# Two zero products for TensorE, K and R scaled by one instruction, and a new order behind the start

## The chip, the cores and the metric

The kernel runs on one core of one Trainium2 chip. The metric is the device time of one execution in microseconds; the kernel before was executed three times and the median counts. Traces come from one more execution under the profiler; its span runs from the first to the last instruction of the program.

## The reference: what is computed

Two layers follow one another.

The first is a linear attention with decay: batch 4, 8 heads, 768 steps, head width 48. For each head a 48 x 48 state is carried along the steps:

```python
cur   = einsum('bhd,bhe->bhde', u * k[t], v[t])
y[t]  = einsum('bhd,bhde->bhe', r[t], state + cur)
state = w * state + einsum('bhd,bhe->bhde', k[t], v[t])
```

The second takes y as x, 3072 rows of 384: `h = relu(x @ w_in)` (384 to 1024 columns), a convolution over three neighbouring steps per column, `gate = sigmoid(conv)`, and `(h * gate) @ w_out` (1024 to 384). The inputs come as 64-bit numbers for the two weight matrices and the convolution, as float32 otherwise.

## The kernel before, in words

**The attention part** works on 24 groups (6 for each batch) of 128 steps, each group two chunks of 64 steps. For each group g `load` issues the transfers of K and R with the head width on the partitions (one tile `KR`, K in its half 0, R in its half 1), of K and R with time on the partitions (`KV`), and of V. `prep` (line 379) scales K and R by powers of the decay: two VectorE products (lines 384 to 386, recorded under the helper's line 208), each of 112 x 512 elements, one for K by `TK`, one for R by `TR`. `TK` and `TR` are the halves of one tile, `TKR`, which ScalarE and VectorE fill at the start (lines 320 to 323). For g below 4 `prep` also transposes K with small TensorE products ("kt", line 394) and sums u*k*r with others ("q", line 407); later groups do this on VectorE and GpSimd. Then come three families of small TensorE products, all recorded under line 495: scores (K by R, into `psA` or a bank lent by the other layer), additions to the state (K by V), and outputs (`psY`, scores by V and R by state). For g below 4 they are the separate operations VA, VU and VY, later one operation V of 64 or so interleaved products. `chain` masks the scores into `RS` (line 512) and carries the state (`SS`, `SD`); `split` cuts y into a high and a low part for the second layer (`XT`, lines 549 and 550).

**The second layer** runs in 7 units of up to 510 steps, 8 blocks of 128 columns each, so 56 blocks. `first(i)` makes 9 TensorE products (line 581) of up to 512 columns into one of two banks `HP`. ScalarE takes the relu and the middle tap (lines 585, 586), VectorE the two outer taps (line 589), ScalarE the sigmoid (592), VectorE the product with h (593), ScalarE the high part `GH` (595) and VectorE or GpSimd the low part `GL`. The bank is free for block i + 2 when line 593 has read it. `second(i)` makes three times 3 products (line 610) into the three banks `PO`, which are copied out and stored after the eighth block. The 16 weight pieces are converted from 64-bit numbers along the way (lines 349 to 365).

**The start** is a list of its own: `warm` (line 274) makes 40 products of a zero tile `wz` into banks that nobody uses yet, 5 with 512 columns and 35 with 104.

**What sets the order.** Each call of `op` records an operation with its engines, an assumed duration and what it reads and writes. Nothing is scheduled in the kernel: `Plan.order` reads the list `ORDER`, one number for each operation, with a letter where an operation that may run on several engines gets one (a: ScalarE, d: VectorE, p: GpSimd). The operations are then issued in that order, and each engine works through its own share of it, first in, first out. All transfers are issued by SyncE, in the order of the list too.

Of the kernel before, what the change touches and what calls it, by code (L numbers as in the profile page):

```python
# [11 lines left out]
ALU = mybir.AluOpType  # L12
# [4 lines left out]
C = 64  # L17
NP = H // 2
# [34 lines left out]
FN = 256  # L53
# [3 lines left out]
26 17 0 8 12 15 10 1 16 4 21 14 9 5 27 11 20 2 23 18 22 43 13 33 35 19 3 31 44 37 32 50 34 55 82 38 56 81 28 39 64 29  # L57
59d 40 41 36 72 57 6 30 73 60 76d 45 77 46a 52d 58a 47 208 74 207 48 61 7 49d 84a 65 51 63d 83 78 62a 85 230 80p 214
88 66 67 229 68a 53 42 75d 54 69p 103 90 210a 70 104 86 209 92d 107d 236 89 211 100 91 212 108 71a 87d 215 213d 105 93
109 79a 216d 110p 232a 95d 276 112 217 106a 277 111d 231 113 98 126 96 233 94a 97p 218 127 115 237 219p 283 114 116a  # L60
238d 124 99 299 24 234 25 117 239 298 278 279d 125 131 118a 240 280 119a 241d 235d 140 155d 121 123 281 158d 101 130
149 120 150 134p 122 102 132 146 148 285a 147 284 156d 198 301a 343 286 300 282d 305 133a 302 287 344 220 153 199 129
154 200 128 303 201 350 135 304p 221 202 152 222 138 157 142p 136 203 223 288p 137a 139 204 224 175p 267 143 170 173
151 225 144a 176p 226 141 268 289 159p 269 145 177 307a 270 227 160 162p 306 271 346a 369 308 272 174 169 290 273 345
205 228d 375 334 291 347 171 352a 206d 368 166 163 292 351 164p 168 313 167 274 178p 413 312 335 165 172 309 161 311
182p 336 357 293 275p 348 180 337 294 179a 349p 338 295 353 356 189 310d 339 359 193d 256 370 340 196p 187 184 181 188
371a 358 183 194p 377a 431 185 404 296 186 191 376 360 192 414 361 297d 242 405 378 354 372 406 362 355p 373 407 382
381 379 247 383 258 259 363 248 195 251 253 249 252 364 341 365 262p 374p 419 420 422 254 250 190 257 197p 408 342d
437 438 421 439 415a 380d 416 244 245a 409 366 433a 432 423 367p 470 471 469 410 411 424 243 263d 425 426 427 264 246
266a 324 323 255 428 434 260 329d 261 332d 460 461 417 462 463 464 472 435 473 474 475 476 465 466 412p 265p 314 322  # L70
393 325 326 418p 483 316p 330p 331 429 320 321 315 317 327 328 318d 319 430p 436p 482 481 513 525 522 528 399d 400p
333a 477 514 515 516 517 478 384 396 392 450 449 394 401 531 386p 526 523 518 467 390 387 388a 519 520 391 385 532 533
398 389 397 534 535 468p 541 561 402p 440 503 451 452 395 502 448 479 562 563 564 536 529 537 565 480p 538 566 442p
453 454 443 446 403a 540 542 573 572 521p 584 574 575 508d 567 604 605 606 444p 445 447 441 682 455p 494 576 458p 484
492 504 530 501 490 456p 457 607 608 577 491 578 579 568 569d 486a 487 509p 511p 539p 570 571 583 582 615 616 617 618
459p 493 506 507 488p 489 614 626 613 625 627 485 543 609 619 610 545d 556p 580 581d 658 510 620 621 497 505 496 495
499 524 500 498 648 551 550 599p 659 557d 555 554 622 512a 547 611 612p 649 650 546 544 548 623 651 652 558 653 549
593 594 654 598 660 661 662 663 664 559p 670 585 592 552 597 600p 624p 665 587 590 666 701 702 703 655 671 713 719 657
669 588p 560p 589 591 601 603a 586 602p 553 527 595 628 636 704 705 720 706 641 656d 721 707 722 723 637 691 596 638
690 714 630p 631 632d 716 729 710 717 724 634 667 711 751 752 753 725 763 668d 643d 629 635 761 694 708 764 765 754  # L80
755 642 728 730 762 633 646d 672 689 692 726 756 757 758 795 644p 709p 674p 766 767 768 746p 696p 678 679 645 683 688
685 640 741 686 693 639 687 675 684 740 759d 647a 796 797 769 770 773 774 760 772 807 808 809 727p 805 673 676d 798
744 799 800 680 677 697d 698 695 681 817 806 804 747p 749p 699p 733p 810 801 811 812 731 737 784 739 745 813 748 734
735a 771d 837 838 839 814 849 700p 738 736 732 777d 840 790d 793p 791p 850 841 851 842 852 843 802 803d 775 789 778
816 818 888 848 847 846 779p 815p 788 853 792 844 750a 854 855 889 890 781 776 794d 780 782 845d 906 907 908 856 909
742 712 715 827 821p 743 819 859 858 860 903 900 910 820 911 912 891 823 913 892 783 785 830 893 822 894 950 897 938
951 952 895 832p 833d 834 835d 826 883p 886p 857p 831 824 896p 953 954 955 787 786 861 901 939 868 866 877 828 825 878
718 956 836p 862 940 881 941 942 867 873 871 876 872 870 928 829 927 898 863 904 994 995 915 947 917 916 943 944 945
884d 946d 885 864d 882 865 982 1176 957 958p 914p 996 983 984 985 986 932 997 933d 987 988 869 887a 948 960 959 949
961 991 993 1003 918 924 934p 920p 998 936d 935 977d 980p 999 1000 1001 879 992 1004 880 899 874 875 1026 1038 921  # L90
922p 931 919 923 1027 1028 937p 964d 925 962 1036 926 930 971 972 902 929 1029 1030 1039 1031 989 990p 978p 1002d 1032
1040 1041 1042 965 976 966d 1043 979 1074 1035 1005 1037 1049 1044 1095 1091 1047 1033 1075 1076 968 1077 975 1078 969
1079 967 963 1096 1097 1080 1098 1034p 1021p 1016 905 1015 973 974 970 1006 1012 1008p 981p 1014 1007 1009 1010d 1099
1100 1081 1045 1020 1011 1019 1101 1046d 1024p 1069d 1070p 1060 1048 1087 1083 1088 1017 1092 1093 1084 1107 1108 1102
1109 1125 1110 1013 1071 1111 1126 1127 1112 1082d 1113 1128 1129 1106 1105 1117 1104 1114 1050 1073p 1056 1086 1089
1137 1116 1130 1057 1131 1103p 1149 1134 1146 1138 1139 1072d 1022d 1140 1141 1094 1064 1090 1085 1061 1132 1150 1058
1151 1142 1143 1052p 1068 1133d 1152 1053 1153 1115p 1154 1155 1158 1135 1147 1062 1063 1065 1066 1118 1144 1145p 1159
1171 1161 1162 1163 1023 1025d 1164 1165 1059 1067 1136 1148 1160 1183 1166 1193 1167 1184 1195 1054p 1055 1018 1051
1119 1185 1156 1121d 1186 1157p 1172 1170 1207 1192 1204 1187 1188 1189 1213 1196 1168 1197 1198 1199 1200 1122 1123
1190 1208 1214 1169p 1120 1124 1173 1215 1205 1174 1201 1225 1194 1210 1223 1175 1179 1206 1216 1217 1218 1222 1219  # L100
1237 1191p 1234 1235 1226 1227 1211 1220 1202 1228 1229 1221p 1230 1231 1238 1239 1240 1241 1203d 1249 1250 1251 1252
1242 1243 1253 1224 1244 1232 1254 1247 1246 1236 1248 1233d 1255 1245d 1256 1261 1259 1262 1263 1264 1265 1266 1267
# [56 lines left out]
def rwkv_ffn_kernel(tc, krd, krt, vt, wd, ut, w_in, conv_w, w_out, out):  # L159
# [3 lines left out]
    op = plan.op  # L163
    with ExitStack() as ctx:
# [496 lines left out]
        for i in range(NU * NF + LAG):  # L661
            x = (i + LEAD) / NF
# [80 lines left out]
```

## Time and profile before

| what | value |
|---|---|
| runs shown, us | 294.24, 296.36, 297.02 (median 296.36) |
| profiled execution, its own time | 296.27 us |
| its span, first to last instruction | 294.5 us |
| TensorE (PE) busy | 280.2 us, 95% |
| VectorE (DVE) busy | 242.0 us, 82% |
| ScalarE (ACT) busy | 191.5 us, 65% |
| GpSimd (POOL) busy | 114.8 us, 39% |
| moved by DMA | 37.47 MB, mean 127 GB/s |
| mean granted clock of TensorE | 0.994 |

Busy time is the time in which an instruction of the engine runs; TensorE's is of matrix products alone, its weight loads (PEld) overlap with them. The ends of products are modelled, so a short wait between two can hide in a busy stretch. "Issue" is a wait for which the profile shows no cause. A granted clock of 1.00 is 2.4 GHz, 0.50 is 1.2 GHz.

### The profile page before, as it was taken

Reading aid. Unit: us, or ns where it says so; the run is one execution under the profiler, and the core shown is the slowest. Engines: PE = TensorE matmul, PEld = TensorE weight load, DVE = VectorE, ACT = ScalarE, POOL = GpSimd, SP = SyncE. Lnnn points to the kernel's source line nnn. Section 1 sums busy time; section 2 is a strip of 40 time slices with the busy share of each in tenths; the row PEclk is TensorE's granted clock in tenths of the full one; section 3 lists DMA queues with packets and bytes.
Section 4 is the critical chain, followed back from the end, with each engine's and each line's share of the span. In section 5 each row is a group of like instructions: output and inputs, shape, how many; then the busy total and the mean of one; then the engine's idle time right before and its main releaser. Section 6 shows DMA issues by size and latency. Waiting matters only on the chain.

```text
span 294.5 us, 10385 instructions
## 1 busy us (share of the span) xinstructions
PE 280.2 (95%) x4368; PEld 242.6 (82%) x4368; DVE 242.0 (82%) x439; ACT 191.5 (65%) x452; POOL 114.8 (39%) x143
## 2 busy tenths in 40 slices
PE   8769799999999999998999999999999999999995
PEld 6669788889989988886888878888888888889895
DVE  5867999999998989998997987888798973565561
ACT  3446699997887566866496566464853555656662
POOL 4112164565577635166337333645150340112100
PEclk9979999999999999999999999999999999999999
DMA  7987998977455673435364508643413001200121
GB/s 174 225 193 198 234 227 227 241 167 176 120 159 161 168 199 118 118 82 154 90 202 129 157 2 186 191 147 87 146 44 61 2 4 45 92 0 0 38 71 56
DMA packets 18642, 37.47 MB, mean 127 GB/s; under 512 B 3874, under 2 KB 10532, under 8 KB 18596
## 3 DMA queue, kind: packets, MB, share of 16 engines
q1 hardware_dynamic: 18596, 36.82, 48.0%
q8 instruction: 34, 0.56, 0.8%
q14 instruction: 12, 0.10, 0.1%
HBM read 30.01 MB, written 4.72 MB: 118 GB/s over the span
## 4 chain that ended last, share of the span: by engine, by line
PE 46%; DVE 18%; issue 9%; ACT 9%; POOL 7%; DMA 7%; SPq 4%; POOLq 0%; ACTq 0%
PE PO L610 17%; PE HP L581 16%; DVE CV L589 6%; PE psY L495 5%; SPq L212 4%; DMA KV<-in_krt_dram 4%; POOL KV L208 4%; DMA ST<-in_w_in_dram 3%; DVE SG L593 2%; POOL GL L208 2%; DVE KR L208 2%; ACT CV L586 2%; DVE XT L550 2%; ACT HP L585 1%; ACT SG L592 1%
## 5 line engine op out<-in xcount | busy, mean ns | idle before, releaser
L581 PE MATMUL HP<-XT,wi 128*128 128x512 f32 (+3 forms) x504 | 111.5, 367 | 2.9 <-DVE SG L593 1.4
L581 PEld LDWEIGHTS HP<-XT,wi 128*128 128x128 f32 x504 | 88.0, 188 | 18.6 <-DVE SG L593 3.7
L610 PE MATMUL PO<-GH,wo 128*128 128x510 f32 (+3 forms) x336 | 101.9, 363 | 0.0
L589 DVE SCALAR_TENSOR_TENSOR CV<-HP,cw,CV 128x510 f32<-128x510 f32 (+3 forms) x112 | 74.9, 672 | 17.6 <-ACT CV L586 15.8
L610 PEld LDWEIGHTS PO<-GH,wo 128*128 128x128 f32 x336 | 61.4, 188 | 8.6
L208 POOL TENSOR_TENSOR GL<-SG,GH 128x510 fp32r<-128x510 f32 (+3 forms) x31 | 36.4, 1175 | 66.1 <-ACT GH L595 64.2
L610 PE MATMUL PO<-GL,wo 128*128 128x510 f32 (+3 forms) x168 | 60.6, 361 | 0.0
L592 ACT ACTIVATE SG<-CV 128x510 f32<-128x510 f32 (+3 forms) x56 | 32.0, 571 | 43.0 <-DVE CV L589 42.7
L495 PE MATMUL psY<-RS,KV 64*48 64x64 f32 x720 | 42.9, 220 | 0.4 <-issue 0.4
L593 DVE TENSOR_TENSOR SG<-HP,SG 128x510 f32<-128x510 f32 (+3 forms) x56 | 34.2, 611 | 11.0 <-ACT SG L592 10.3
L585 ACT ACTIVATE HP<-HP 128x512 f32<-128x512 f32 (+3 forms) x56 | 29.4, 525 | 19.3 <-PE HP L581 16.8
L495 PE MATMUL psY<-KR,SS 48*48 48x64 f32 x660 | 39.8, 215 | 1.1 <-issue 1.1
L595 ACT CAST GH<-SG 128x510 fp32r<-128x510 f32 (+3 forms) x56 | 30.7, 554 | 8.5 <-DVE SG L593 7.3
L586 ACT ACTIVATE CV<-HP,cw 128x510 f32<-128x510 f32 (+3 forms) x56 | 35.1, 628 | 1.3
L610 PEld LDWEIGHTS PO<-GL,wo 128*128 128x128 f32 x168 | 31.6, 188 | 3.7
L208 DVE TENSOR_TENSOR KR<-KR,TKR 112x512 f32<-112x512 f32 x48 | 34.2, 724 | 0.1
L495 PEld LDWEIGHTS psY<-RS,KV 64*48 64x48 f32 x720 | 31.9, 120 | 0.9 <-issue 0.9
L495 PEld LDWEIGHTS psY<-KR,SS 48*48 48x48 f32 x660 | 30.2, 119 | 1.2 <-issue 1.2
L495 PEld LDWEIGHTS psA<-KR 48*64 48x64 f32 x704 | 22.3, 135 | 6.5 <-issue 2.6
L495 PE MATMUL psA<-KR 48*64 48x64 f32 x704 | 25.2, 221 | 0.2
L505 POOL TENSOR_TENSOR SD<-SS,PW 112x192 f32<-112x192 f32 x21 | 14.3, 681 | 24.5 <-DVE SS L526 8.5
L431 ACT ACTIVATE RS<-eye,QQ 128x64 f32<-128x64 f32 x80 | 20.2, 336 | 2.0 <-DVE QQ L415 2.0
(113 smaller groups left out, 351.9 us busy)
## 6 DMA issues: line engine op xcount, KB each, us to landing
KR<-in_krd_dram SPq DMA_DIRECT2D x24, 448.0 KB, 4.9
KV<-in_krt_dram SPq DMA_DIRECT2D x40, 192.0 KB, 4.2
KV<-in_vt_dram SPq DMA_DIRECT2D x48, 96.0 KB, 4.3
ST<-in_w_in_dram SPq DMA_DIRECT2D x16, 192.0 KB, 5.3
ST<-in_w_out_dram SPq DMA_DIRECT2D x8, 384.0 KB, 6.9
XT<-XT SPq DMA_DIRECT2D x24, 64.0 KB, 2.7
out_dram<-OS SPq DMA_DIRECT2D x6, 255.0 KB, 3.3
out_dram<-OS SPq DMA_DIRECT2D x3, 251.0 KB, 2.1
```

Source lines behind the costliest of these rows:

```text
L208: op(eng, d, rd, wr, lambda e: e.tensor_tensor(**kw), cls, port=True)
L431: A.activation(RS[j][:, n], eye, AF.Copy, scale=QQ[j][:, n:n + 1])
L495: PE.matmul(y, a, b_, start=s0, stop=s1)
L505: e.tensor_tensor(out=dst, in0=src, in1=PW[:, :, 64:65].broadcast_to([112, NP, D]), op=ALU.mult)
L581: PE.matmul(hp, wi[a][:, j, fs], XT[:, x, j, t], start=(j == 0 and k == 0), stop=(j == 2 and k == 2))
L585: op("act", 0.093 + n / 1200.0, [], [H_], lambda e: A.activation(hp, hp, AF.Relu, scale=1.0 / WS))
L586: op("act", 0.158 + n / 1200.0, [H_, "cw"], [("T", ti)], lambda e: A.activation(t1, hp[:, 1:n + 1], AF.Copy, scale=cw[:, 3 * f + 1:3 * f + ...
L589: op("dve", 0.117 + n * 1.085e-3, [H_, "cw"], [("T", ti)], lambda e, k=k: V.scalar_tensor_tensor(out=t1, in0=hp[:, k:n + k], scalar=cw[:, ...
L592: op("act", 0.11 + n / 1200.0, [("T", ti), "sgt"], [("SG", ti)], lambda e: A.activation(sg, t1, AF.Sigmoid))
L593: op("dve", dps(n), [H_], [("SG", ti)], lambda e: V.tensor_tensor(out=sg, in0=hp[:, 1:n + 1], in1=sg, op=ALU.mult), "GG")
L595: op("act", act(n), [("SG", ti)], [("GH", gi)], lambda e: A.copy(gh, sg))
L610: PE.matmul(PO[m][:, :n], wo[a][:, f, ms], g2[x], start=(f == 0 and k == 0), stop=(f == NF - 1 and k == 2))
```

## The change

Three edits, in one step.

1. `FILL = 2` operations are recorded right behind `warm`: each is one product of the zero tile, 128 x 128 by 128 x 512, into the bank `PO[2]`. In the new list the first stands between the second "q" and the second "kt" product group, the second between VA and VU of group 2.
2. In `prep` the two products for K and R become one product of 112 x 1024 elements, which reads all of `TKR` and so waits for all four parts of it. There are 24 such operations in place of 48.
3. The list `ORDER` is another one. With the numbers resolved to operations, the lists of the engines agree at the beginning: SyncE's first 53 transfers are the same in the same order; TensorE's first 29 operations are the same but for the two inserted ones; VectorE's first 80 or so are the same, where the merged product mostly stands at the place of the first of the two. Behind that, from about 47 us on, blocks, visits and transfers stand in another order, and some operations change their engine: in the whole list VectorE has 396 operations (433 before), ScalarE 369 (360), GpSimd 133 (129), TensorE 269 (267), SyncE 204 (204).

```diff
-FN = 256
+FN, FILL = 256, 2
 ...
 ORDER = """
-26 17 0 8 12 15 10 1 16 4 21 14 9 5 27 11 20 2 23 18 22 43 13 33 35 19 3 31 44 37 32 50 34 55 82 38 56 81 28 39 64 29
 ...
+19 0 28 14 8 17 10 9 1 18 23 4 16 5 13 29 22 25 20 2 24 15 45 21 37 3 35 33 46 39 34 52 36 82 57 81 40 30 42 41 65 31
 ...
 """
 ...
         op("pe", 2.6, ["wz"], ["o2", "o0", "psY", "psU", ("HP", 1)], warm, "warm", 6144)
 
+        for k in range(FILL):
+            op("pe", 0.2133, ["wz"], ["o2"], lambda e: PE.matmul(PO[2][:, :512], wz[:, :128], wz, start=True, stop=True), "fill", 512)
+
 ...
             kt, rt = ([(n_, i, o) for o in (0, 64)] for n_ in ("Kt", "Rt"))
-            for x, W, key, ks in ((0, TK, "K", ["TK1", "TK2"]), (1, TR, "R", ["TR1", "TR2"])):
-                v = KR[i][:, x].rearrange("q p (c t) -> q p c t", c=2)
-                tt("dve", 512, ks, [(key, i)], "KR", out=v, in0=v, in1=W.unsqueeze(2).broadcast_to([112, NP, 2, C]), op=ALU.mult)
+            v = KR[i].rearrange("q x p (c t) -> q (x p) c t", c=2)
+            tt("dve", 1024, ["TK1", "TK2", "TR1", "TR2"], [("K", i), ("R", i)], "KR", out=v, in0=v,
+               in1=TKR.rearrange("q x p t -> q (x p) t").unsqueeze(2).broadcast_to([112, 2 * NP, 2, C]), op=ALU.mult)
```

## Rows read from the trace of the kernel before

**Rows 1.** Stretches: PE, PEld, DVE, ACT, POOL busy (count), clock, DMA share, GB/s.
```profile
0.00:47.00 47.00, 39.24 (x984) 35.92 (x984) 38.20 (x82) 29.02 (x83) 14.93 (x34) 0.96 0.89 209
47.00:100.00 53.00, 51.67 (x985) 48.36 (x976) 51.14 (x99) 44.99 (x122) 33.94 (x39) 1.00 0.68 174
100.00:200.00 100.00, 98.47 (x1560) 81.51 (x1559) 90.00 (x156) 65.12 (x144) 44.95 (x49) 1.00 0.52 139
200.00:291.30 91.30, 90.81 (x854) 76.83 (x852) 62.69 (x105) 51.98 (x103) 21.01 (x23) 1.00 0.15 45
291.27:294.50 3.23, 0.00 (x0) 0.00 (x0) 0.00 (x0) 0.39 (x1) 0.00 (x0) 1.00 0.32 110
```

**Rows 2.** Timeline of PE: start, us, instructions, [idle before <- releaser].
```profile
15.94 0.49 PE L394 MATMUL HP<-DW,KR 48*64 48x48 f32 x9 [3.15 <-issue]
22.14 0.26 PE L495 MATMUL psY<-KR,SS 48*48 48x64 f32 x2 [1.09 <-issue]
30.83 0.21 PE L495 MATMUL PO<-RS,KV 64*48 64x64 f32 x1 [1.28 <-issue]
```

**Rows 3.** Stretches between and in PE's gaps of the start, columns as in rows 1.
```profile
12.80:15.94 3.14, 0.00 (x0) 0.00 (x0) 2.32 (x4) 0.73 (x4) 1.64 (x2) 1.00 1.07 231
15.94:21.06 5.12, 5.11 (x127) 4.96 (x127) 3.57 (x8) 2.06 (x7) 0.52 (x1) 0.67 0.76 165
16.60:20.00 3.40, 3.40 (x82) 3.40 (x78) 2.44 (x6) 1.97 (x6) 0.52 (x1) 0.50 0.84 183
22.14:25.69 3.55, 3.54 (x127) 3.46 (x128) 2.50 (x7) 1.12 (x4) 0.26 (x1) 1.00 0.43 135
30.83:34.59 3.76, 3.76 (x127) 3.63 (x127) 3.59 (x8) 1.47 (x5) 0.79 (x1) 1.00 0.89 223
```

**Rows 4.** The page: PE's busy us and instructions; the queue's packets, MB, share.
```profile
PE 280.2 (95%) x4368; PEld 242.6 (82%) x4368; DVE 242.0 (82%) x439; ACT 191.5 (65%) x452; POOL 114.8 (39%) x143
q8 instruction: 34, 0.56, 0.8%
```

**Rows 5.** The same queue from 12.8 to 15.94 us.
```profile
q8 instruction: 1, 0.02, 2.8%
```

**Rows 6.** Timeline of the warm-up's products; then the 512-column products of line 581.
```profile
1.69 0.63 PE L274 MATMUL psU<-wz 128*128 128x512 bf16 x1
2.12 0.63 PE L274 MATMUL HP<-wz 128*128 128x512 bf16 x1
...
L581 PE MATMUL HP<-XT,wi 128*128 128x512 f32 x288 | 72.4, 397 | 1.5 <-ACT CV L586 0.9 <-DVE SG L593 0.4 <-DMA XT<-XT 0.2
```

**Rows 7.** VectorE's products under line 208: ns min/median/max, first and last start.
```profile
L208 DVE TENSOR_TENSOR KR<-KR,TKR x48: 674/682/1980, 5.6 to 232.3; 112x512 f32<-112x512 f32 x48
L208 DVE TENSOR_TENSOR wi<-TT,wi x5: 544/550/559, 12.2 to 36.3; 128x384 fp32r<-128x384 f32 x5
```

**Rows 8.** Timeline around the first scalings of K and R.
```profile
5.49 0.30 ACT L323 COPY TKR<-TKR 112x128 f32<-112x128 f32 x1 [0.26 <-DVE TKR L320]
5.56 1.29 DVE L208 TENSOR_TENSOR KR<-KR,TKR 112x512 f32<-112x512 f32 x2
7.54 1.15 PE L495 MATMUL psA<-KR 48*64 48x64 f32 x32
8.61 0.68 DVE L208 TENSOR_TENSOR KR<-KR,TKR 112x512 f32<-112x512 f32 x1
9.30 0.17 DVE L318 TENSOR_TENSOR uw<-HP,wc 48x4 f32<-48x4 f32 x1
9.77 1.14 PE L407 MATMUL psY<-uw,KP 48*64 48x64 f32 x32
```

**Rows 9.** Waits from 47 us on: us in total, times, longest.
```profile
PE HP L581 <- DVE SG L593: 1.2, 3, 0.5
PE HP L581 <- ACT CV L586: 0.9, 1, 0.9
PEld psA L495 <- DVE KR L208: 1.2, 3, 0.5
```

More of the change, by code (lines that the diff above doesn't have):

```diff
@@ L61 @@
[L61 to L65, printed above, removed]
@@ new lines @@
+462 460 310p 259p 415 416 417 418 255 425a 407a 406 408 403 419 424 426 409 410p 247 244 246 248 245 451 308 254 252
+250 317 404p 258 387 316 420 463 474 461 472 473 452 453 427 311 454 455 322d 421 422d 456 312a 457 260p 464 465 466
+313 467 468 309 469 503 504 505 470 321 314 315 428p 515 516 518 512 458 513 519 521 522 506 507 508 323p 325p 324
+326a 523 253 319 386 318 320 377 459d 530 509 390 550 383 551 552 379p 471p 391p 380 381p 394p 392p 446p 449p 378 382
+434a 384 524 559 532 525 526 553 393 554 527 510 432 531 435 438 555 439 395p 556 511p 560 562 592 571 436a 437 385
@@ new lines @@
+760 770 725 772 701 729 704 771 768 769 811 833 834 823 824 825 826 798 835 776 836 735d 766 787p 837 761 763 838 773
+827 828p 764p 765 802 801 830 870 839 871 872 805a 873 874 767 831 842 888 829 799p 882 843 889 890 891 777p 803 809
+813 860 810 875 876 815p 816p 892 807 806 808 877 893 894 778d 818d 698 919 841 879 920 921 922 923 931 883 898 885
+932 814 804 844 861 863 812 840p 878p 933 924 865p 866p 868p 925 962 886 880 926 927p 846 847a 849 934 864 817 935 850
+853 859 857 856 910 854 855 858 909 914d 899 895 963 964 936 965 929 897 930 928 937 974 851 819a 917p 896p 867 852
@@ new lines @@
+1182 1183 1180 1181p 1172 1188 1203 1189 1204 1205 994 1046 1194 1038 1195 1202 1097 1200 1196 1206 1197 1215 1207
+1169p 1186 1101 1208 1100 1102 1098 1151 1212 1216 1217 1152 1198 1209 1227 1218 1219 1153 1201 1220 1221 1228 1210
+1229 1222 1230 1211d 1231 1199p 1232 1239 1214 1226 1213 1224 1240 1241 1233 1234 1225 1237 1236 1248 1238 1190 1155
+1160 1158 1184 1157 1159 1187 1156 1242 1243 1251 1244 1235p 1245 1263 1223p 1260 1250 1252 1253 1264 1254 1255 1265
+1256 1257 1258 1266 1267 1268 1269 1249 1262 1246 1275 1276 1277 1259d 1247d 1278 1279 1270 1271p 1280 1281 1272 1296
@@ L109 @@
+1297 1298 1299 1274 1261 1308 1284 1300 1301 1302 1309 1310 1282 1311 1312 1285 1292 1293 1313 1273 1288 1289 1290
+1303 1305 1320 1314 1321 1322 1323 1324 1306 1332 1283p 1304d 1325 1326 1317 1307 1318 1330 1333 1315 1334 1335 1336
+1327 1337 1344 1329 1319 1341 1331 1342 1345 1346 1338 1339 1328p 1316p 1353 1343 1354 1357 1355 1347 1348 1349 1350
+1340p 1360 1351 1352d 1365 1295 1286 1294 1287 1291 1366 1367 1356 1359 1362 1358 1363 1361 1364 1368 1369 1370
 """
```

77 lines of the change are left out of this document (31 added, 46 removed).

## The prediction, made before the result was known

> **What bounds the kernel now.** I read the table of stretches first, then the waits and the timeline of TensorE, then the queues. The stretches [rows 1] show two regimes. Before 47 us TensorE's products are busy 39.24 us of 47.00; from there to its last product at 291.3 us they are busy in all but 1.33 + 1.53 + 0.49 = 3.35 us, and the last 3.23 us are copying and storing out. So behind 47 us the products themselves are the bound, no order can win more than these 3.35 us and what little hides between products, and VectorE stands close behind (51.14 of 53.00 us between 47 and 100). What is large is idle in the start.
>
> The timeline shows what that idle is: TensorE stops in the middle of groups of small products for 3.15, 1.09 and 1.28 us, each time with "issue" as releaser [rows 2], so no other engine is waited for. The stretches between the gaps tell the cause [rows 3]: 127 products and 127 or 128 loads, then a stop, three times over. The page has 4368 products and 4368 loads, and 34 packets with 0.56 MB on the queue named instruction [rows 4]: 8736 / 34 = 257 instructions and 16.5 KB for each packet. One such packet falls in the gap from 12.80 to 15.94 us [rows 5]. I read these gaps as TensorE waiting for its next block of instructions. Where the DMA engines are at a share of 1.07 the gap is 3.15 us; where they are at 0.43, from 22.14 to 25.69, the stop behind is too short to stand among the three [rows 3].
>
> Now the clock. It stands at 0.50 (1.2 GHz) from 16.60 to 20.00 us and at 1.00 elsewhere in the rows [rows 3]; before it fell TensorE had been idle from 12.80 to 15.94. In these 3.40 us it was busy throughout and did the work of 1.70 us at 2.4 GHz. But the work ends at 21.06, in front of the next gap, which lasts until 22.14. If that gap ends when the block lands, a faster clock only makes it longer.
>
> Here a rule of the Trainium skill speaks otherwise. "Runtime: NRT & Kernel Launch", section Instruction fetch mechanics, says that the sequencer refills in 16 KiB blocks of 256 instructions while it executes, and that crossing a block border is mostly hidden. The trace agrees with the block's size and differs on the hiding: 3.15 us. By the rule the gaps would have another cause, nothing would fix their ends, and the sum below would hold -1.70 us for the clock in place of 0; that result is the first rival.
>
> **The change part by part.** The sum is made against the profiled execution, 296.27 us for a span of 294.5; the median of the runs shown, 296.36, is 0.09 above it.
>
> *The two zero products.* One costs between 0.25 us (72.4 us / 288 products of 512 columns) and 0.43 us (from 1.69 to 2.12 in the warm-up, at half the clock) [rows 6]; two cost 0.50 to 0.86. The first stands just ahead of the 3.15 us gap, the second, between VA and VU of group 2, ahead of the one that ends at 30.83; both only use up gap [rows 2], and they wait for nothing. I take 0; without that cover 0.86. Their four instructions move the block borders by two and four instructions, nothing at some 28 ns a product (3.55 us / 127) [rows 3].
>
> *What they give back in the clock.* Nearest row: 3.40 us at half clock [rows 3], worth up to -1.70. The first fill runs ahead of the gap and does not shorten the idle time of 12.80 to 15.94 by more than itself, so I expect the clock to fall as before in most executions. And if it does not, TensorE comes to the next border at 21.06 - 1.70 = 19.4 and waits there. I take 0, between -1.70 and +1.70: the upper end is a second fall of the same size, since 22.14 - 19.4 = 2.7 us of idle would then stand where 1.09 is now.
>
> *K and R by one instruction.* The medians of 682 ns for 512 elements and 549 for 384 [rows 7] give 1.04 ns an element and about 150 ns that do not depend on the size. One product of 1024 elements is then 150 + 1065 = 1.21 us, against 1.36 for two; the bounds are 1.18 (from the shortest, 674 and 544: 1.02 ns an element) and 1.36 (nothing saved). VectorE is relieved by some 0.15 us for each of 24 groups, 3.6 in all. At the start the product must wait for all of TKR, whose last part ends at 5.79; it then ends at about 7.0 to 7.2, still ahead of the scores at 7.54 [rows 8]: 0. The second group's product runs from 8.61 to 9.82, so uw, at 9.30 now, comes at about 9.85 and "q", at 9.77 now, a quarter of a microsecond late [rows 8]; the 3.15 us gap behind it takes that up: 0.
>
> *The order behind 47 us, and the relief of VectorE.* VectorE gets 433 - 396 = 37 operations less, 24 of them from the merging, ScalarE and GpSimd 13 more between them; TensorE's own work stays. The bounds are the idle time there: -3.35 if all of it goes, +3.35 if it doubles. Of TensorE's waits there 1.2 us end with line 593 on VectorE and 0.9 with line 586 on ScalarE [rows 9]. The relief acts on the first kind alone: I take -1.2. ScalarE, which gets nine operations more, is late next.
>
> *The moved transfers.* SyncE's first 53 are the same; behind them the order differs, where the DMA share is 0.68 and lower [rows 1]. No row shows TensorE waiting there long for a transfer: 0, within the bounds above.
>
> Sum: 0 + 0 + 0 - 1.2 = -1.2, so 296.27 - 1.2 = **295.1 us**.
>
> **The rivals.**
>
> *The clock counts (faster).* The gaps are not fixed in time, or the fills hold the clock, and the 1.70 us of the slow stretch come off in full; with 1.2 to 2.3 from the order this is 293.4 to 292.3. For it: the fall is the only one in the trace, in a stretch without any idle. Against it: the gap of 1.09 us right behind it, and the fill's place ahead of the idle time. Chance 0.22.
>
> *The long scaling holds VectorE (slower).* A block of 1.21 us stands where VectorE could slip something in after 0.68. Ahead of line 593 it makes the bank HP free up to 0.5 us later, and TensorE's next nine products wait; three such waits are there now [rows 9], and VectorE has only 1.86 us to spare between 47 and 100 [rows 1]. 18 of the 24 scalings lie behind 47 us (36 of the 48 products now). At 0.5 us each it decides from about nine: 9 x 0.5 = 4.5, less the 1.2, gives 299.6; all of them would give 304. Against it: of the two products now, both must be done before the scores may start (1.2 us of load waits for KR [rows 9]), so the pair is needed together anyway, and the new list was written for the long form. Chance 0.15.
>
> *The clock falls in a worse place.* It holds at 16.6, TensorE idles 2.7 us ahead of 22.14, and the 3.55 us behind that run at half the clock, where the next border follows at once: +1.7, with the order's -1.2 about 296.8. Chance 0.13.
>
> *Nothing happens.* The order gives nothing, the relief lies beside TensorE's work: 296.3. Chance 0.15.
>
> **How the numbers follow.** The forecast, about 294 to 296, has 0.35. About 1% (2.96 us, so 293.4 and 299.3) is what a measurement of this kernel can tell from no change. Faster by over 1% is the first rival: 0.22. Slower by over 1% is the second: 0.15. Within 1% are the forecast and the two others: 0.63. The range reaches from 292.6, which cuts off the far end of the first rival (about half of it), to 298.6, above which the second lies with little else: 1 in 10 and 1 in 10 left out.
>
> **What would show it.** Right: three gaps of about 3, 1 and 1.3 us still ahead of the 128th product or so, with "issue"; the fills beside them; KR x24 at 1.2 us; TensorE's start stretch as long as now to within half a microsecond; the waits on line 593 below 1.2 us. If the clock stays at 1.00 and the next gap has grown by as much, the reading of the gaps holds; if the gap has not grown and everything behind stands 1.7 us earlier, it is wrong. Wrong the other way: new waits of line 581 on line 593 with a KR ahead of it, or on ScalarE. A transfer order that shortens the first gap would make it wrong too, as would a new list that fills the 3.35 us nearly whole.

## The result, and the profile after

The changed kernel takes 297.85 us (median of 20 runs, 295.96 to 301.19), the kernel before in the same comparison 295.98 (20 runs). The ratio is 1.0068, 95% interval 1.0045 to 1.0091: slower by 0.7%, where 0.4% faster was forecast. (The ratios in this document leave out executions more than 1.5% above the fastest of the same kernel and the medians do not, so a ratio is not the quotient of two medians.) The time lies inside the range of the prediction and its sign is the other one. The profiled execution took 298.51 us for a span of 296.6.

The first view is the table of stretches of the changed kernel (columns as in [rows 1]).

```profile
0.00:47.00 47.00, 39.52 (x960) 36.11 (x966) 38.04 (x76) 29.14 (x83) 15.54 (x34) 0.96 0.86 210
47.00:100.00 53.00, 50.72 (x1008) 48.04 (x997) 50.35 (x88) 44.94 (x121) 36.50 (x43) 1.00 0.66 173
100.00:200.00 100.00, 98.62 (x1561) 81.61 (x1560) 88.81 (x140) 69.89 (x167) 51.41 (x48) 1.00 0.50 136
200.00:293.30 93.30, 92.76 (x859) 77.52 (x857) 60.83 (x101) 53.85 (x112) 22.46 (x23) 1.00 0.17 49
293.30:296.60 3.30, 0.00 (x0) 0.00 (x0) 0.00 (x0) 0.39 (x1) 0.00 (x0) 1.00 0.24 83
```

TensorE's last product ends at 293.30 instead of 291.27 [rows 1], so 2.03 of the 2.1 us between the spans lie ahead of it. The start is alike. From 47 to 100 us TensorE is busy 50.72 us, 0.95 less than before, and GpSimd (the fifth pair) 36.50 instead of 33.94; between 100 and 200 it is 51.41 instead of 44.95. Over the whole execution the page puts it like this.

```profile
PE 281.6 (95%) x4368; PEld 243.3 (82%) x4370; DVE 238.0 (80%) x402; ACT 198.2 (67%) x480; POOL 125.9 (42%) x146
```

Against [rows 4] VectorE is busy 4.0 us less and GpSimd 11.1 us more. The relief of VectorE is there; the time is not. Both differences hold stalls too, as will be seen.

The start, in TensorE's timeline and in the stretches between its stops (columns as in [rows 2] and [rows 1]):

```profile
16.44 0.49 PE L396 MATMUL HP<-DW,KR 48*64 48x48 f32 x10 [3.03 <-issue]
21.83 0.32 PE L497 MATMUL psY<-KR,SS 48*48 48x64 f32 x4 [0.33 <-issue]
30.48 0.26 PE L497 MATMUL PO<-RS,KV 64*48 64x64 f32 x2 [0.83 <-issue]
```
```profile
16.44:21.50 5.06, 5.06 (x127) 4.91 (x127) 4.00 (x7) 2.46 (x8) 0.52 (x1) 0.66 0.60 152
17.08:20.49 3.41, 3.41 (x83) 3.41 (x80) 2.93 (x6) 1.97 (x6) 0.52 (x1) 0.50 0.65 174
```

The stop of 3.15 us [rows 2] is one of 3.03 behind the fill, again 127 products lie behind it, and the clock again stands at 0.50 (1.2 GHz) for 3.41 us, as in [rows 3]. So here the fills did not hold the clock; e7 below shows what they cost.

What is new stands in the waits from 47 us on (total, times, longest; answers to [rows 9]).

```profile
PE psA L497 <- DVE KR L207: 1.7, 1, 1.7
PE PO L612 <- DVE GL L207: 1.2, 2, 1.0
PE HP L583 <- DVE SG L595: 0.5, 2, 0.3
PEld psA L497 <- DVE KR L207: 2.5, 2, 2.1
```

The wait that the forecast wanted shorter, HP for VectorE's SG, did fall, from 1.2 to 0.5, and the one for ScalarE's CV is gone. Two others have come: a score that waits 1.75 us for the scaled K and R, and a product of `second` that waits 1.02 us for a low part `GL`. TensorE's timeline at the two:

```profile
95.11 0.27 PE L497 MATMUL psA<-KR 48*64 48x64 f32 x2 [1.75 <-DVE KR L207]
...
101.94 0.44 PE L612 MATMUL PO<-GL,wo 128*128 128x386 f32 x1 [1.02 <-DVE GL L207]
```

VectorE at the same time (start, duration):

```profile
91.61 3.45 DVE L207 TENSOR_TENSOR KR<-KR,TKR 112x1024 f32<-112x1024 f32 x1
...
99.00 2.89 DVE L207 TENSOR_TENSOR GL<-SG,GH 128x386 fp32r<-128x386 f32 x1
101.81 1.21 DVE L207 TENSOR_TENSOR KR<-KR,TKR 112x1024 f32<-112x1024 f32 x1
```

And GpSimd:

```profile
91.53 0.52 POOL L507 TENSOR_TENSOR SD<-SS,PW 112x192 f32<-112x192 f32 x1
92.01 1.02 POOL L207 TENSOR_TENSOR KV<-KV,uu 128x384 f32<-128x384 f32 x1
92.98 1.00 POOL L207 TENSOR_TENSOR KV<-KV 128x384 f32<-128x384 f32 x1
93.92 0.11 POOL L299 MEMSET XT<- 128x8 f32 x1
94.06 1.86 POOL L207 TENSOR_TENSOR KV<-KV,uu 128x384 f32<-128x384 f32 x1
...
98.52 1.02 POOL L207 TENSOR_TENSOR KV<-KV,TH 128x384 f32<-128x384 f32 x1
99.50 1.02 POOL L207 TENSOR_TENSOR KV<-KV 128x384 f32<-128x384 f32 x1
100.47 1.00 POOL L207 TENSOR_TENSOR GL<-SG,GH 128x386 fp32r<-128x386 f32 x1
```

Read the three together. The same scaling takes 1.21 us at 101.81, with GpSimd idle, and 3.45 at 91.61, where it starts 0.08 us behind an SD product of GpSimd, in a row that is unbroken until 93.98. It ends at 95.06, 1.08 us behind the end of that row: it did its work when the row was over. In turn GpSimd's next product, at 94.06, takes 1.86 us instead of 1.02. `GL` at 99.00 does the same behind the row that ends at 101.47. Each time TensorE, which needs the result next, stands still. VectorE's records show no wait: the stall is inside the duration, under the word busy.

VectorE is not always held for a whole row. At 174.09 a scaling starts 0.09 us behind a product of GpSimd and ends 1.08 us behind the end of that one product (175.01); here GpSimd's next product waits, 2.28 us in place of 1.29:

```profile
174.09 2.00 DVE L207 TENSOR_TENSOR KR<-KR,TKR 112x1024 f32<-112x1024 f32 x1
```
```profile
174.00 1.01 POOL L207 TENSOR_TENSOR KV<-KV,TH 128x384 f32<-128x384 f32 x1
174.97 2.28 POOL L207 TENSOR_TENSOR GL<-SG,GH 128x510 fp32r<-128x510 f32 x1
```

What decides between the two outcomes no run shows.

All scalings and all products of line 591, whose input `HP` lies in PSUM (ns min/median/max):

```profile
L207 DVE TENSOR_TENSOR KR<-KR,TKR x24: 1209/1217/3449, 5.8 to 245.4; 112x1024 f32<-112x1024 f32 x24
L591 DVE SCALAR_TENSOR_TENSOR CV<-HP,cw,CV x112: 487/739/752, 38.7 to 287.9; 128x510 f32<-128x510 f32 x64, 128x382 f32<-128x382 f32 x16, 128x386 f32<-128x386 f32 x16, 128x266 f32<-128x266 f32 x16
```

The median of KR is the 1.21 us of the forecast; five of the 24 are drawn out, to 3.45 at most. None of the 112 products with an operand in PSUM exceeds 0.752, though 67 of them run beside a GpSimd product.

To see where the 2.1 us arose I add up TensorE's products in the order of its list, each at the duration that it has when nothing holds it up (28.5 ns for a small one, 0.453 ns a column and 1 ns for one of the second layer), and set the trace's clock against this sum. The work from the 84th to the 96th microsecond (93 to 103 us of the trace) takes 3.14 us longer than in the kernel before, all other stretches together 1.0 us less. So the loss is this one place. The two lists mix small and long products differently, so the sum is an estimate: set against another stretch of the list it moves by up to 1 us.

### The profile page after: what moved, and what is told of

Its sections match the earlier page's. It is cut to its first block, busy times and chain, and to the rows that moved or that the text cites. A ratio compares the mean times of both kernels' runs of the same rounds, so it can differ in the third digit from the quotient of the medians.

```text
span 296.6 us, 10371 instructions
## 1 busy us (share of the span) xinstructions
PE 281.6 (95%) x4368; PEld 243.3 (82%) x4370; DVE 238.0 (80%) x402; ACT 198.2 (67%) x480; POOL 125.9 (42%) x146
## 4 chain that ended last, share of the span: by engine, by line
PE 69%; DVE 18%; ACT 8%; issue 3%; ACTq 0%; DVEq 0%
PE PO L612 25%; PE HP L583 25%; PE psY L497 8%; DVE CV L591 6%; DVE KR L207 4%; PE psA L497 2%; PE psU L497 2%; DVE GL L207 2%; ACT CV L588 2%; DVE SG L595 2%; ACT SG L594 2%; PE PO L273 1%; ACT HP L587 1%; PE psU L396 1%; DVE XT L552 1%
## 5 line engine op out<-in xcount | busy, mean ns | idle before, releaser
L612 PE MATMUL PO<-GH,wo 128*128 128x510 f32 (+3 forms) x336 | 103.4, 365 | 0.0
L207 POOL TENSOR_TENSOR GL<-SG,GH 128x510 fp32r<-128x510 f32 (+3 forms) x38 | 46.4, 1228 | 77.1 <-ACT GH L597 66.9
L207 DVE TENSOR_TENSOR KR<-KR,TKR 112x1024 f32<-112x1024 f32 x24 | 33.8, 1408 | 0.4 <-ACT TKR L325 0.4
L436 POOL TENSOR_SCALAR_AFFINE_SELECT RS<-QQ 64x512 f32<-64x512 f32 x18 | 14.1, 786 | 29.1 <-DVE QQ L417 19.0
L497 PE MATMUL psU<-KV 64*48 64x48 f32 x672 | 20.0, 208 | 0.6 <-issue 0.3
```

The costliest lines, as they stand in the source:

```text
L207: op(eng, d, rd, wr, lambda e: e.tensor_tensor(**kw), cls, port=True)
L436: G.affine_select(out=RS[j][o:o + 64], in_=QQ[j][o:o + 64].unsqueeze(2).broadcast_to([64, NP * 2, C]), pattern=[[0, NP * 2], [1, C]], comp ...
L497: PE.matmul(y, a, b_, start=s0, stop=s1)
L612: PE.matmul(PO[m][:, :n], wo[a][:, f, ms], g2[x], start=(f == 0 and k == 0), stop=(f == NF - 1 and k == 2))
```

## The experiments

Expectations stand as they were written; their letters name the theories open at the time. Ratios are to the kernel before, run in turn with each.

| run | ratio | 95% interval | median us |
|---|---|---|---|
| e1_merge_only | 1.0159 | 1.0113 to 1.0205 | 299.0 |
| e2_merge_and_fill | 1.011 | 1.0063 to 1.0156 | 297.61 |
| e3_no_fill | 1.012 | 1.0078 to 1.0163 | 297.82 |
| e4_split | 1.0225 | 1.017 to 1.028 | 301.14 |
| e5_changed_again | 1.008 | 1.0044 to 1.0117 | 297.63 |
| e6_pool_apart | 1.005 | 1.0009 to 1.0092 | 297.48 |
| e7_fill_only | 0.9998 | 0.9968 to 1.0029 | 295.17 |
| e8_merge_late | 1.0032 | 0.9998 to 1.0066 | 296.42 |
| e9_pool_apart_2 | 1.0069 | 1.0031 to 1.0108 | 297.02 |
| e10_old_order_clean | 1.0076 | 1.0039 to 1.0113 | 297.78 |
| e11_short_warmup | 1.0044 | 0.9998 to 1.0089 | 298.18 |
| e12_kt_on_dve | 1.0023 | 0.9985 to 1.0062 | 296.0 |
| e13_changed_memset / e18, the same again | 0.9925 / 0.9912 | 0.9891 to 0.996 / 0.9866 to 0.9959 | 292.84 / 293.14 |
| e14_before_memset / e16, the same again | 0.9917 / 0.9959 | 0.9886 to 0.9948 / 0.9923 to 0.9994 | 292.13 / 292.97 |
| e15_old_order_clean_memset / e17, the same again | 1.0001 / 0.9986 | 0.9969 to 1.0033 / 0.9948 to 1.0023 | 294.91 / 294.41 |

### The three parts, one at a time

**e1, e2:** the old order with the merged product at the place of the first of the two, without and with the fills.

```diff
-FN = 256
+FN, FILL = 256, 0        # e2: 256, 2, at the places of the change
-            for x, W, key, ks in ((0, TK, "K", ["TK1", "TK2"]), (1, TR, "R", ["TR1", "TR2"])):
...
+            tt("dve", 1024, ["TK1", "TK2", "TR1", "TR2"], [("K", i), ("R", i)], "KR", out=v, in0=v,
...
```

> The order of before, with each pair of K and R products replaced by the one long product at the place of the first; no zero products, nothing else moved. Theory O (the new order costs the time, by where it puts GpSimd's products against VectorE's): no loss, 0.996 to 1.002 of before. Theory M (the long product holds VectorE too long): slower, 1.004 or more. Theory F (the zero products cost it): as theory O.

> The order of before with the long product and with the two zero products at the places that the change gives them; only the new order behind 47 us is left out. Theory O: 0.996 to 1.002 of before, and about 2 us faster than the changed kernel. Theory M and theory F: 1.004 or more. The clock may fall once or not at all; if the clock matters, runs at a granted clock of 0.998 or more are 1.7 us faster than those at 0.994.

Both slower, 1.6 and 1.1%, their intervals overlapping: the merging costs in the old order, as theory M has it and theory O does not. A part of it may be the place. Group 3's product stands where K's stood, and GpSimd's product KP of that group takes 2.93 us in e1 and 2.92 in e2, where it takes 1.27 in the kernel before and in the changed one. The next "kt" waits 2.22 and 1.97 us for the state; but waits of 1.2 to 2.5 us stand there in other executions too, whose stops were short, so this wait is no proof. e10 below takes that place away.

**e3, e4:** the changed kernel without the fills, and with the merging undone (two products, one right behind the other).

```diff
-FN, FILL = 256, 2
+FN, FILL = 256, 0        # e3
```
```diff
-            tt("dve", 1024, ["TK1", "TK2", "TR1", "TR2"], [("K", i), ("R", i)], "KR", out=v, in0=v,
...
+            for x, W, key, ks in ((0, TK, "K", ["TK1", "TK2"]), (1, TR, "R", ["TR1", "TR2"])):   # e4
...
```

> The changed kernel without its two zero products, everything else as changed. Theory O: still 1.004 to 1.010 of before. Theory M: the same. Theory F: back at 0.998 to 1.002.

> The changed kernel with its new order and zero products, but K and R scaled by two products of 512 that stand one behind the other. Theory O: still 1.004 to 1.012 of before, with some 3.6 us more of VectorE's time. Theory M: back at 0.998 to 1.002.

Without the fills it is 1.2% slower than before, the fills no part of it. With two short products in the new order it is the slowest of all, 2.25%, above the ranges of both theories, so the long form is not what costs in this order. The line of VectorE's timeline that answers to 91.61 above:

```profile
90.18 4.31 DVE L208 TENSOR_TENSOR KR<-KR,TKR 112x512 f32<-112x512 f32 x2
```

The two take 4.31 us at the same place of the list, behind the same row of GpSimd. TensorE's waits for KR are 3.0 us there, 2.6 the longest. At this place the row of GpSimd decides, not the length of VectorE's instruction.

**e7:** the kernel before with the two fills alone. **e8:** the old order, merged from group 5 on, the start as before.

```diff
-FN = 256
+FN, FILL = 256, 2        # e7: nothing else but their two places in ORDER
```
```diff
+            if g < 5:     # e8
                 for x, W, key, ks in ((0, TK, "K", ["TK1", "TK2"]), (1, TR, "R", ["TR1", "TR2"])):
...
+            else:
+                tt("dve", 1024, ["TK1", "TK2", "TR1", "TR2"], [("K", i), ("R", i)], "KR", out=v, in0=v,
...
```

> The kernel before with the two zero products alone. My prediction's view (the gaps of the start wait for instructions, the products lie in their cover): 0.998 to 1.002. If the clock counts and they hold it: 0.994 to 0.997, and granted clocks of 0.998 or more in most runs. If they cost: 1.002 to 1.004.

> The order of before, long product for group 5 and later, two products as before for the first five groups; no zero products. The one that had the long product everywhere came out at 1.016 and its profile behind the start was 1.8 us longer than before. Theory S (the long product also costs time in the start, by what it delays there): 1.004 to 1.008. Theory that all of it lies behind the start: still 1.012 or more.

The fills: 0.9998, nothing to 0.3%. The late merging: 0.3% slower with an interval that touches 1, below both expected ranges and undecided by itself. Its trace decides more: counted as above, the part behind the start is some 2.3 us longer than before, about as in e10 below.

### The collision, taken away by moving work

**e5** is the changed kernel once more. **e6** moves two of the KV products that make up the row at 91.6 to VectorE, `GL` at 99.00 to GpSimd, and the third KV product behind the scaling.

> The changed kernel once more, so that it stands on the same chip as the three others. All theories: 1.004 to 1.010 of before.

```diff
 # ORDER, numbers as in the changed kernel: 447, 498 are KV products, 529 is GL, 499 the third KV product, 479 an SD
-442 441 433 477p 447p 498p 669 499p 389 388 445 475 ... 481 448 595 ... 450a 529d 602 ... 615 614 479p 497
+442 441 433 477p 669 389 388 445 447d 475 ... 481 448 498d 499p 595 ... 450a 479p 529p 602 ... 615 614 497
```

> The changed kernel with one stretch put right: around 91 to 102 us of its trace two products of u and k leave GpSimd for VectorE and one product GL goes the other way, so that no row of GpSimd products runs into the long K and R product and into GL. Theory O: the K and R product at 91.6 takes about 1.7 us or less in place of 3.45, TensorE's waits of 1.75 and 1.02 us go, and the time falls by 2 to 3 us, to 0.996 to 1.002 of before. Theory M: no change against the changed kernel (within 0.7 us).

e5 gives 1.008, and its trace again has a scaling of 3.46 us and `GL` of 2.88 at this place: the collision belongs to the list, not to one execution. e6 takes the first one away (1.52 us) and gains nothing that the intervals separate, because the next scaling collides. VectorE's and GpSimd's timelines of e6:

```profile
95.93 5.27 DVE L207 TENSOR_TENSOR KR<-KR,TKR 112x1024 f32<-112x1024 f32 x1
```
```profile
95.69 0.52 POOL L507 TENSOR_TENSOR SD<-SS,PW 112x192 f32<-112x192 f32 x1
96.16 1.03 POOL L207 TENSOR_TENSOR GL<-SG,GH 128x386 fp32r<-128x386 f32 x1
97.14 1.03 POOL L207 TENSOR_TENSOR KV<-KV,TH 128x384 f32<-128x384 f32 x1
98.12 1.03 POOL L207 TENSOR_TENSOR KV<-KV 128x384 f32<-128x384 f32 x1
99.09 1.03 POOL L207 TENSOR_TENSOR GL<-SG,GH 128x386 fp32r<-128x386 f32 x1
```

Five products in an unbroken row that ends at 100.12, and the scaling ends at 101.20, again 1.08 us behind it: 5.27 us, 4.06 of it lost. TensorE's wait for RS, which stands behind it on VectorE, is 2.0 us.

**e9** goes further: beside e6's moves the next KV products and a `GL` go to VectorE too.

```diff
 # ORDER, against e6
-476 501p 533 ... 607 608 609 502a 545p 570p 548d
+476 501d 533 ... 607 608 545d 609 502a 548d 570d
```

> The changed kernel with both collisions taken apart: as the first try, and three more GpSimd products behind them (one KT, one KRT, one GL) go to VectorE, so that GpSimd has nothing to do while the second long K and R product runs. Theory C (a product on VectorE that finds GpSimd busy waits until GpSimd's row of products ends, however long the row): no K and R product above 2.6 us between 80 and 110 us of the trace, no wait of TensorE above 0.7 us there, and 2 us less than the changed kernel: 0.998 to 1.003 of before. Rival (the order is slow for another reason): 1.005 or more.

No scaling is longer than 2.36 us and no wait of TensorE for one is left; for SG and GL it waits 1.0 us each. Yet the ratio is 1.0069, with an interval much like that of the changed kernel, in the rival's range. The work taken off GpSimd lies on VectorE now, and what the stretch from 84 to 96 gains (2.3 us in the trace) the next one gives back in part (1.1). Moving products about did not settle the question.

**e10:** the whole start of the changed kernel, the old order behind it, merged product.

```diff
 # ORDER of the kernel before; merged product and fills at the changed kernel's places up to 47 us,
 # behind that each merged product at the place of the first of the two
```

> The first 47 us exactly as in the changed kernel (long product at its places, zero products), the order of before behind them, with the long product at the place of the first of the two. It takes the changed kernel's new order away and nothing else. If the new order is what costs: 0.998 to 1.003. If the long product alone costs as much in the old order: 1.005 to 1.010, and the new order is no loss. From the profiles of the earlier variants behind 48 us I expect 1.5 us of loss against before there: 1.004 to 1.006.

As slow as the changed kernel (1.0076), so in the old order too the merged product costs behind the start. VectorE's and GpSimd's lines at the place that loses most:

```profile
126.94 2.28 DVE L207 TENSOR_TENSOR KR<-KR,TKR 112x1024 f32<-112x1024 f32 x1
```
```profile
126.85 1.29 POOL L207 TENSOR_TENSOR GL<-SG,GH 128x510 fp32r<-128x510 f32 x1
```

The scaling starts 0.09 us behind a `GL` of GpSimd and ends at 129.22, once more 1.08 us behind the end of GpSimd's product (128.14). TensorE then waits 0.7 us for a KV product and, at 139.20, 1.52 us for ScalarE's CV, where it waits 0.93 in the kernel before. In that kernel the two short products of this group start at 127.12 and 129.16 and take 0.68 us each; the first starts ahead of GpSimd's `GL` (127.51 to 128.95), the second behind it, and between them run two products of line 589, which read PSUM. So the long form loses here by its place beside GpSimd, though GpSimd has no more to do than before.

**e12:** the kernel before with two of its KV products on VectorE, to take away its own longest collision (`GL`, 2.45 us at 135.14).

```diff
-744 799 800 680 677 697d 698 695 681 817 806 804 747p 749p 699p 733p 810 801
+744 799 800 680 677 697d 698 695 681 817 806 804 747p 749d 699d 733p 810 801
```

> The kernel before, where two products by TH for groups 11 and 12 go from GpSimd to VectorE at their places in the list, since they keep one GL of VectorE waiting at 135 us (2.45 us in place of 0.68) and TensorE after it (0.93 us). Theory C: GL takes 0.7 us, that wait goes, 0.7 to 1.1 us are won: 0.996 to 0.998. Rival: VectorE's 1.1 us more are paid elsewhere: 1.000 or more.

1.0023, no difference, as the rival has it: the two collide themselves, and TensorE has new waits of 0.6 and 0.4 us.

### The stops of the start

**e11:** the kernel before with a warm-up of 12 products of 512 columns, 28 products and 28 loads fewer.

```diff
-NBUF, NT, NST, LAG, WPRE, NW, WN = 3, 3, 3, 3, 2, 40, 104
+NBUF, NT, NST, LAG, WPRE, NW, WN = 3, 3, 3, 3, 2, 12, 512
```

> The kernel before with a warm-up of 12 products of 512 columns in place of 5 of 512 and 35 of 104: the same time at half the clock, 56 instructions fewer. Theory I (the stops of the start are block borders of TensorE's instructions): the stops come at the same count of instructions, so 28 products later in the program: the first one not within the second kt group but within the additions or scores behind it, the others 28 products later too. Time: 0.993 to 1.002. Rival (the stops belong to what is computed or loaded there): they stay at the same products.

TensorE's timeline, and the stretch up to its first stop:

```profile
15.51 0.51 PE L495 MATMUL psU<-KV 64*48 64x48 f32 x14 [2.31 <-issue]
20.98 0.70 PE L495 MATMUL HP<-KV 64*48 64x48 f32 x23 [0.53 <-issue]
26.08 0.73 PE L495 MATMUL psU<-KV 64*48 64x48 f32 x18 [1.36 <-issue]
```
```profile
0.00:15.50 15.50, 11.72 (x221) 8.01 (x222) 10.93 (x27) 6.21 (x17) 4.78 (x19) 1.00 0.88 192
```
The same stretch of the kernel before:
```profile
0.00:15.93 15.93, 11.31 (x222) 9.41 (x222) 11.15 (x27) 6.28 (x17) 5.04 (x19) 1.00 0.89 202
```

The stop comes at the same count, 221 products and 222 loads (222 and 222 before), and thereby 28 products later in the work: at `psU<-KV` and no longer at `HP<-DW,KR`. What is waited for is bound to the number of instructions, not to what they do. That is the reading of the prediction, shown. The runs leave open whether the shorter warm-up costs (1.0044, interval touching 1).

The trace of e5 shows what the clock does to these stops. It is the changed kernel once more, with a granted clock of 1.00 (2.4 GHz) throughout the start:

```profile
14.58 0.49 PE L396 MATMUL HP<-DW,KR 48*64 48x48 f32 x10 [1.38 <-issue]
20.06 0.32 PE L497 MATMUL psY<-KR,SS 48*48 48x64 f32 x4 [1.95 <-issue]
```

TensorE is through its 127 products in 3.53 us in place of 5.06 and then stands still for 1.95 us in place of 0.33. The ends of the two stops lie 5.48 us apart, against 5.39 in the execution in which 3.41 us ran at 0.50 (16.44 and 21.83). That is one pair of executions; in all traces that have both stops the distance lies between 4.4 and 6.2 us.

### The collision, taken away as such

In **e13, e14 and e15** GpSimd's two-input products of KV, GL, wi and wo are each replaced by two fillings of the same tile, which read nothing and together take about 0.85 of the time (this part of the computation is left out): in the changed kernel, in the kernel before, and in e10. Engines, order and counts of VectorE and TensorE stay. **e16, e17 and e18** are the same three again, in another comparison.

```diff
+            def product(e):
+                if e is G and cls in ("KRT", "KRU", "KT") or e is G and wr[0][0] in ("GL", "wi", "wo"):
+                    o = kw["out"]
...
+                    for _ in range(2):
+                        G.memset(o, 0.0)
+                else:
+                    e.tensor_tensor(**kw)
-            op(eng, d, rd, wr, lambda e: e.tensor_tensor(**kw), cls, port=True)
+            op(eng, d, rd, wr, product, cls, port=True)
```

> The changed kernel, in which GpSimd's products KRT, KRU, KT, GL and its low parts of the weights are left out: two fills with zero of the same output stand in place of each, about as long. Order, waits and VectorE's work are as in the changed kernel. Theory C (the loss is VectorE's two-input products waiting for rows of GpSimd's two-input products): the long K and R products take 1.2 us nearly everywhere (none over 2 us), the time falls by at least 2 us against the changed kernel, and it ends within 0.4% of the same edit in the kernel before. Rival (the new list or the long product is slow by itself): the difference of 0.7 to 0.8% between the two stays.

> The same edit in the kernel before: the same GpSimd products left out and replaced by two fills each. Theory C: somewhat faster than before, 0.990 to 0.998, since it has collisions too (2.45 us for a GL at 135 us, 1.98 for a K product). Rival: no change, 0.999 to 1.001.

> The same edit in the variant with the changed kernel's start, the long product and the order of before behind (1.0076). Theory C: within 0.4% of the other two with this edit. If the long product costs by itself in the old order, it stays 0.5% or more above the kernel before with this edit.

> As e14: the kernel before with GpSimd's two-input products replaced by two fillings each (their part of the computation left out). What is open: the medians of e14 and e15 differ by 0.84%, but behind the start (from 48 us of TensorE's work on) the two traces differ by 0.2 us only. Theory D (what the long product costs are GpSimd's rows and nothing else; the difference of the medians stands in the start of the executions): ratio 0.992 to 0.997, less than 0.4% from e17, and behind the start within 0.3 us of e17 and e18. Rival (the long product costs by itself in the old order, as the second rival of the prediction says): 0.992, and e17 again 0.7 to 0.9% above it.

> As e15: old order behind the changed start, long product, GpSimd's two-input products replaced by fillings (part of the computation left out). Theory D: within 0.4% of e16 and e18, behind the start within 0.3 us of both. Rival: 1.000, 0.7 to 0.9% above e16, with waits of TensorE behind VectorE's long products in the trace.

> As e13: the changed kernel with GpSimd's two-input products replaced by fillings (part of the computation left out). Theory D: 0.992 to 0.996, and TensorE's waits behind the start no longer than 0.5 us in all. Rival (the new order holds the long product's price down): 0.992, with e17 0.7 to 0.9% above it.

The scalings of e13:

```profile
L214 DVE TENSOR_TENSOR KR<-KR,TKR x24: 1206/1217/1260, 5.8 to 239.2; 112x1024 f32<-112x1024 f32 x24
```

No scaling exceeds 1.26 us any more (the longest of e14 takes 1.13, of e17 1.54). The one that answers to 91.61 starts at 89.46, in VectorE's and GpSimd's timelines:

```profile
89.46 1.21 DVE L214 TENSOR_TENSOR KR<-KR,TKR 112x1024 f32<-112x1024 f32 x1
```
```profile
89.45 1.73 POOL L212 MEMSET KV<- 128x384 f32 x4
```

It runs beside four fillings in its full 1.21 us. And TensorE's waits from 47 us on, all of them in e13:

```profile
PE PO L620 <- POOL GL L212: 0.3, 1, 0.3
PE PO L620 <- DVE GL L214: 0.2, 1, 0.2
```

The 1.7 and 1.2 us are gone. The pages of e13 and e14 show what the stalls had added to VectorE's busy time:

```profile
PE 280.2 (97%) x4368; PEld 242.8 (84%) x4370; DVE 227.0 (78%) x402; ACT 197.9 (68%) x480; POOL 102.4 (35%) x234
```
```profile
PE 280.2 (96%) x4368; PEld 243.5 (83%) x4368; DVE 235.2 (80%) x439; ACT 191.2 (65%) x452; POOL 99.3 (34%) x219
```

With the same instructions VectorE is busy 11.0 us less than in the changed kernel (238.0) and 6.8 less than in the kernel before (242.0). Its relief by the change is 8.2 us without collisions; half of it went into stalls. The times follow. By the sum of TensorE's work used above, from its 72nd microsecond to the last product:

| kernel | as it is | without GpSimd's two-input products |
|---|---|---|
| before | 208.03; with fills (e7) 208.08 | 206.70, 206.41 |
| changed | 211.11; again (e5) 211.08; without fills (e3) 211.03 | 206.82, 206.47 |
| old order, merged (e10) | 210.49 | 207.15, 207.49 |

The changed kernel loses 3.0 us against before in this part, to within 0.1 in three executions; without the products that collide the two differ by 0.1. It gets 4.3 to 4.6 us back, before 1.3 to 1.6. The loss depends on where the part begins (1.7 to 3.7 us), since the lists differ; but wherever it begins, the changed kernel gets back 2.7 to 3.1 us more than the kernel before. The runs agree: pooling the pairs, the changed kernel without them has a mean of 292.4 (21 runs, standard error 0.3), the kernel before 292.9 (18, 0.3), against 297.7 and 294.9 with them. So GpSimd's two-input products account for the whole loss of the changed kernel against the kernel before. The test is not perfectly pure: two fillings of KV take 0.87 us where a product took 1.02, so GpSimd's rows are also somewhat shorter. But GpSimd's own results are hardly waited for in the changed kernel: behind 47 us the waits of TensorE's products do not name it, those of its loads do for 0.2 us and VectorE's for 0.6.

e15 and e17 settle the third row only in part. My expectation wanted each within 0.4% of the other two. e15 is 0.8% above e13 and e14; e17 is 0.3% above e16 and 0.75% above e18, which is what the rival of e18 says (e18 itself, at 0.9912, came out just below its range). Pooled they lie 1.5 us (0.5%, standard error 0.4 us) above e14 and e16. Of that 0.4 to 1.1 us stand behind the start in the traces. So in the old order the long product seems to cost a little without collisions too, and the new order took that away, at most 0.5%, and paid it back in collisions.

## Why the prediction failed

**What held.** TensorE's stops in the start are bound to instruction counts (e11). The fills cost 0 and give 0 (e7: 0.9998). KR takes 1.21 us when nothing meets it (the lower bound of 1.18 should read 1.19). The relief of VectorE by the scalings, put at 3.6 us, is 4.4 without collisions (33.6 us in e14, 29.2 in e13) but 1.0 with them (34.8 before, 33.8 changed; sums of their durations). The moved transfers cost nothing that shows. In the profiled execution the clock fell again at the same place, with the same stop ahead of it; in e5 it did not, and the next stop took up the time, as the prediction had it. That the 0.43 us of a warm-up product were spent at half the clock no row shows: the profile has 1.00 there.

**The step that failed** is "The order behind 47 us, and the relief of VectorE", with its -1.2; in the traces it measured about +3 at one place and -1 elsewhere. "The relief acts on the first kind alone": that wait did fall, from 1.2 to 0.5 us, and ScalarE's 0.9 went too. But "ScalarE ... is late next" named the wrong engine. What cost was GpSimd, which is busy 11.1 us longer [rows 4], and not by being late with its own results but by lying across VectorE's. The prediction counted GpSimd's operations and never asked what runs beside what: it put collisions at nothing, and they cost about 3 us more than before. Nor was the -1.2 fully there beneath them: without the colliding products the changed kernel is 0.5 us faster than the kernel before (292.4 against 292.9, standard error 0.4), and the traces differ by 0.1. Nor can the amount of GpSimd's work alone be the cause: e10 leaves GpSimd's list as it was and is as slow.

The row that could have told it stood in front of me. [rows 7] has KR at 674/682/1980: one of 48 took three times the median, and I used the median. Around that one, in the kernel before, VectorE and GpSimd show

```profile
99.08 2.58 DVE L208 TENSOR_TENSOR KR<-KR,TKR 112x512 f32<-112x512 f32 x2
```
```profile
99.23 0.90 POOL L505 TENSOR_TENSOR SD<-SS,PW 112x192 f32<-112x192 f32 x1 [0.28 <-DVE SS L526]
100.09 1.01 POOL L208 TENSOR_TENSOR KV<-KV 128x384 f32<-128x384 f32 x1
```

the same thing: both engines drawn out, GpSimd's SD product from 0.52 to 0.90, VectorE's second product to 1.98.

The Trainium skill has the rule that spoke against this change: "SBUF — State Buffer", section Who interferes with whom, says that a VectorE instruction with two SBUF inputs contends with a GpSimd instruction that reads SBUF, not with one that only writes it, and that one with at most one SBUF input, outside the modes in which VectorE takes both ports, does not contend. The traces agree with all three: 3.45 us against 1.21 (KR beside products), 1.21 beside fillings (e13), 0.752 at most for the products of line 591. It also says that issue order decides who blocks, and, of those modes, that whoever issues first has the shared pair for the whole instruction. By that KR at 91.61 would have been let in when the SD product ended at 92.05, ahead of the KV products issued at 92.01 and 92.98, for a loss of 0.44 us. The trace has 2.24, until the row of three was over, and that decides; at 174.09 the trace does as the rule says.

**The rivals.** "The long scaling holds VectorE" had the right sign, with 0.15, and the wrong mechanism: it priced 0.5 us nine times in the waits for SG, which got shorter. The loss came in two large pieces in waits for KR and GL. Its size (299.6) was too large by 1.8 us. Against "The clock counts" stands e5: there the clock stayed at 1.00, and the next stop was longer by 1.62 us, nearly the 1.70 that the rival wanted back. "The clock falls in a worse place" and "Nothing happens" were nearer in time (296.8 and 296.3) and are not what happened. What a fall costs in general is not settled. 118 runs of the kernel before, by mean granted clock, have medians of 293.83 (0.998 and above, 19 runs), 294.79 (0.992 to 0.994, 59), 295.12 (0.987 and 0.988, 31) and 296.53 (0.980 to 0.983, 9). So a lower mean clock goes along with 0.3 to 1.4 us from one group to the next; but in the profiled executions a fall mostly followed a long stop, which costs by itself, and no run here separates the two.

Not shown: why VectorE waits for a whole row at 91.61 and for one product at 174.09. No version that computes everything came out faster than the kernel before.

## What to carry to other kernels

Before work is moved from VectorE to GpSimd, or VectorE's instructions are made longer, lay the two timelines over each other: a VectorE product with both inputs in SBUF that meets an unbroken row of GpSimd products can cost the rest of that row (3.45 and 5.27 us for 1.21 here), and at least that of the product under way in the places shown; it appears as busy time. Look at the maximum beside the median of each group, and follow one outlier before the sum is made. Where an order must put the two side by side, put there operations of VectorE with an operand in PSUM, or of GpSimd that only write.

## What was not expected of the hardware

- A VectorE product of 1.21 us lasted 3.45 and 5.27 us behind three and five GpSimd products, and 2.00 behind one. The GpSimd product that lets it pass is drawn out in turn (1.02 to 1.86, 1.29 to 2.28).
- The stops in the start are bound to the count of instructions, but their lengths are not fixed: the first was 3.15 us in the kernel before, 3.03 in the changed one, 2.31 in e11, 0.61 in e1. TensorE came to its 48th microsecond of work between about 55 and 61 us in the traces of the kernels with the full warm-up, while the part behind the 72nd repeats to 0.1 us in the kernels that compute everything (0.4 with the fillings). The runs of the kernel before have a standard deviation of 1.2 us (118 runs), to which the start may add most; so a change of 0.4% in the order has to be read from the trace behind the start, where it stands out, and not from a few medians.
